# Window attention with a SoLU layer on one Trainium2 core: all turned rows in the weights' buffers, more load buffers, a new early list and new homes

## The chip, the cores and the metric

The kernel runs on one NeuronCore of a Trainium2 chip. The metric is the device time of one execution in microseconds; lower is better. Several runs are taken, and their median is quoted. Beside them stands one profiled execution, from which all rows below are read; its time is its own and need not be the median.

## What is computed

The reference is windowed causal attention (window 64, batch 8, 8 heads, sequence 576, head size 64), and its output, as 4608 tokens of 512 numbers, goes through a two-layer block with a softmax-weighted activation and a layer norm:

```python
scores = scale * np.matmul(q, k.transpose(0, 1, 3, 2))
mask = (rel >= 0) & (rel < window)
attn = softmax(np.where(mask, scores, -1e9))
x = np.matmul(attn, v)            # then rows of B*S tokens, 512 wide
h = x @ w_in                      # 512 -> 1024
sm = np.exp(h - h_max); sm = sm / (sm.sum(-1) + 1e-9)
solu = h * sm
ln = (solu - mu) / np.sqrt(var + 1e-6) * g_ln
out = ln @ w_out                  # 1024 -> 512
```

## The kernel before

The 4608 tokens are cut into 36 tiles of 128 rows. A tile t goes through these steps, named by letters in the list `START` and in `course`: S (scores, softmax over eight heads, and from tile 8 on the attention matrix turned by way of DRAM), T (for tiles below 8 the same turn on TensorE), X (attention times v), B (a power-of-two scale for the row block), h and H (the two halves of the product with w_in, then the statistics and the norm, then two 16-bit planes of the result that are stored to DRAM and come back turned by a transposing DMA), M (that turn on TensorE for the tiles that don't go by DMA), and O (the product with w_out and the store). I and G compute the weights' scales and split each 32-bit weight block into a high and a low 16-bit part.

Weights come as 64-bit numbers into the buffers "raw"; ACT and DVE rebuild 32-bit weights from them in eight blocks of tag "w" (`weight_block`): an ACT scaling, the low bits (on POOL or DVE), and two integer steps on DVE. Blocks 0 to 3 are w_in, 4 to 7 w_out. Tiles 0 to 2 multiply with the 32-bit w_in (L840), tile 0 also with the 32-bit w_out (L991). All later products use three 16-bit passes each (L852 for w_in, L1001 for w_out).

The order of instructions is made by a small planner (`Plan`) at build time. Each operation has an engine and an estimated cost; TensorE's operations follow the order of `START` and then of `course`, with those of tiles below `LOOSE` = 3 free to move. Buffers are rings (`RINGS`): an operation on a buffer waits until the earlier user of that slot is done. The planner runs the whole kernel forward by its estimates and writes one fixed order for each engine and for the DMA queue of SP. Ahead of the first output product it fills a share of the gaps that it foresees on TensorE with matmuls of no use (L1080, L1082).

`HOMES` says on which engine each movable operation of each tile runs, with the key (task, tile, part); from tile `LATER` = 14 on, even tiles use key 14 and odd ones key 15. Tasks: "low bits" and "high" for weights, "scale" (the softmax rows times the reciprocal sum; "ALL" is one DVE instruction for four heads), "soft" (the planes of the attention matrix), "join" (v rows of two tiles in one buffer; on SP it is a DMA from DRAM), "norm", "high planes" and "planes" (the two 16-bit planes of the normed rows), "tiny" (one-column arithmetic of the norm) and others. A key that is not listed takes a default, for example DVE for "planes" from tile 3 on and POOL below, ACT for "high planes" and POOL for "soft".

The turned rows of a tile live where `at_Y` says: tile 0 in its own buffer "yF", tiles below `FAR` in the ring "yT", the others in the ring "w" behind the eight weight blocks. `HALVES` names the tiles whose scores, transposes and values are cut into two pieces of four heads. The ring "pH" in PSUM has one buffer: a tile's product with w_in can't start until ACT's exponential and DVE's product (L876) of the tile before have read it. The largest |v| of a tile (L520 on DVE) needs the tile's v load.

Of the kernel before, what the change touches and what calls it, by code (L numbers as in the profile page):

```python
# [55 lines left out]
FAR = 8  # L56
# [16 lines left out]
    ("join", 8, 0): "POOL", ("join", 8, 1): "DVE", ("join", 9, 1): "DVE", ("join", 10, 0): "SP",
    ("join", 11, 0): "SP", ("join", 11, 1): "POOL", ("join", 12, 0): "SP", ("join", 12, 1): "DVE",
    ("join", 13, 1): "SP", ("join", 15, 0): "SP", ("low bits", 0, 0): "DVE", ("low bits", 2, 0): "DVE",
    ("low bits", 3, 0): "DVE", ("low bits", 6, 0): "DVE", ("norm", 0, 0): "DVE", ("norm", 0, 1): "DVE",
    ("norm", 1, 1): "DVE", ("norm", 2, 0): "DVE", ("norm", 3, 1): "DVE", ("norm", 5, 0): "DVE",
    ("norm", 6, 0): "DVE", ("norm", 9, 0): "DVE", ("norm", 10, 1): "DVE", ("norm", 11, 0): "DVE",
    ("norm", 11, 1): "DVE", ("norm", 13, 1): "DVE", ("norm", 14, 0): "DVE", ("norm", 14, 1): "DVE",
    ("norm", 15, 0): "DVE", ("norm", 15, 1): "DVE", ("planes", 1, 0): "DVE", ("planes", 2, 0): "DVE",  # L80
    ("planes", 2, 1): "DVE", ("planes", 3, 1): "POOL", ("planes", 4, 1): "POOL", ("planes", 5, 0): "POOL",
    ("planes", 5, 1): "POOL", ("planes", 6, 0): "POOL", ("planes", 7, 0): "POOL", ("planes", 7, 1): "POOL",
    ("planes", 8, 0): "POOL", ("planes", 8, 1): "POOL", ("planes", 9, 0): "POOL", ("planes", 10, 0): "POOL",
    ("planes", 10, 1): "POOL", ("planes", 11, 0): "POOL", ("planes", 12, 0): "POOL", ("planes", 13, 0): "POOL",
# [186 lines left out]
def tile_window_attention_solu_moe(  # L271
# [856 lines left out]
```

## Time and profile before

| | before |
|---|---|
| median of 3 runs | 500.72 us (500.54 to 501.61) |
| the profiled execution | 502.51 us |
| its span, from the first to the last instruction | 500.7 us |
| mean granted TensorE clock | 1.000 |
| TensorE busy | 490.8 us, 98% of the span |
| ACT, DVE, POOL busy | 375.5, 372.2, 174.5 us |
| DMA queue of SP: share of 16 engines | 82.0% |

The profile gives the busy time of each engine, which waits ended last before an instruction and by whom they were ended, and the chain of work that ended last. TensorE has a gap only where an input comes late; the filler matmuls count as busy.

### The profile page before, as it was taken

The numbers are of one execution on the slowest core, as the hardware profiler recorded it, in microseconds if no ns is written. First come the engines' busy times: TensorE is split into PE (matmuls) and PEld (weight loads), VectorE is DVE, ScalarE is ACT, GpSimd is POOL, SyncE is SP. The second block draws the span as 40 slices with busy tenths as digits, with TensorE's granted clock in tenths as the row PEclk, the third lists the DMA queues.
The fourth block names the chain that finished last, engine by engine and source line by source line (L and its number), as shares of the span: only waits on it lengthen the run. The fifth ranks groups of instructions, "written<-read, shape, count | busy, mean of one in ns | idle before, by whom it ended". The sixth has DMA issues, their size and how long they took to land.

```text
span 500.7 us, 12038 instructions
## 1 busy us (share of the span) xinstructions
PE 490.8 (98%) x4263; PEld 264.3 (53%) x4263; DVE 372.2 (74%) x1300; ACT 375.5 (75%) x1053; POOL 174.5 (35%) x302
## 2 busy tenths in 40 slices
PE   8999999989999999999999999999999999999997
PEld 7566654544555555545454545454545454444453
DVE  5998998888875869777778777788787887556440
ACT  4989999587977787988787878787878697543340
POOL 1255232534684342453333322232323242422100
PEclk9999999999999999999999999999999999999999
DMA  8982342769999999999999999999999999963311
GB/s 346 404 324 86 105 150 62 178 189 272 260 267 271 294 290 196 312 265 284 265 264 258 215 269 283 257 265 257 230 294 265 289 252 198 226 157 106 107 40 44
DMA packets 159292, 113.90 MB, mean 227 GB/s; under 512 B 130240, under 2 KB 130496, under 8 KB 158720
## 3 DMA queue, kind: packets, MB, share of 16 engines
q1 hardware_dynamic: 154912, 105.27, 82.0%
q10 hardware_dynamic: 4320, 7.87, 4.9%
q8 instruction: 33, 0.54, 0.5%
q14 instruction: 27, 0.22, 0.2%
HBM read 39.72 MB, written 41.42 MB: 162 GB/s over the span
## 4 chain that ended last, share of the span: by engine, by line
PE 80%; SPq 7%; DVE 5%; DMA 4%; issue 2%; ACT 1%; POOL 0%; POOLq 0%; ACTq 0%
PE pO L1001 28%; PE pH L852 27%; PE pS L671 5%; PE pX L808 5%; PE pH L840 4%; SPq L946 3%; SPq L754 3%; PE pX L1001 2%; DMA yd<-pl 2%; DMA yT<-yd 2%; PE pO_sums L448 2%; PE pO_x L808 2%; PE pO L991 1%; PE t L777 1%; PE t_s L671 1%
## 5 line engine op out<-in xcount | busy, mean ns | idle before, releaser
L852 PE MATMUL pH<-w_inH,xH 128*128 128x512 f16 x528 | 162.0, 379 | 0.4 <-DVE mst L888 0.4
L1001 PE MATMUL pO<-w_outH,w 128*128 128x512 f16 x416 | 128.1, 379 | 0.0
L852 PEld LDWEIGHTS <-xH 128*128 128x128 f16 x792 | 75.5, 98 | 90.4 <-issue 1.6
L692 ACT ACTIVATE sS<-sS,nmx 128x128 f32<-128x128 f32 x288 | 112.1, 398 | 7.3 <-DVE nmx L687 7.0
L1001 PEld LDWEIGHTS <-w 128*128 128x128 f16 x672 | 64.6, 98 | 77.5 <-issue 1.2
L852 PE MATMUL pH<-w_inL,xH 128*128 128x512 f16 x264 | 99.0, 379 | 0.0
L1001 PE MATMUL pO<-w_outL,w 128*128 128x512 f16 x208 | 78.8, 379 | 0.0
L873 ACT ACTIVATE e<-pH,mst,xscale 128x1024 f32<-128x1024 f32 x33 | 39.7, 1203 | 34.0 <-DVE mst L871 33.6
L867 DVE TENSOR_REDUCE mst<-pH 128x1 f32<-128x1024 f32 x36 | 44.0, 1222 | 24.7 <-PE pH L852 21.5
L692 ACT ACTIVATION_READ_ACCUMULATOR sS<-sS,nmx 128x1 f32 x288 | 56.7, 197 | 0.0
L876 DVE CUSTOM_DVE_ANT_0 e<-pH,e 128x1024 f32<-128x1024 f32 x36 | 44.0, 1222 | 10.4 <-ACT e L873 10.3
L937 POOL TENSOR_TENSOR pl<-e,pl 128x512 f16<-128x512 f32 x37 | 43.0, 1177 | 21.8 <-ACT pl L934 20.9
L880 ACT ACTIVATE unread<-e,mst 128x1024 bf16<-128x1024 f32 x36 | 41.2, 1144 | 11.3 <-DVE mst L879 10.7
L901 DVE TENSOR_SCALAR e<-e,mst 128x512 f32<-128x512 f32 x56 | 30.0, 573 | 20.4 <-POOL mst L896 18.7
L687 DVE CUSTOM_DVE_ANT_0 sS<-pS,maskNone 128x128 f32<-128x128 f32 x168 | 38.5, 286 | 7.4 <-PE pS L671 6.7
L895 POOL TENSOR_TENSOR mst<-mst,neghalf 128x1 f32<-128x1 f32 x36 | 20.1, 559 | 68.3 <-DVE mst L893 58.5
L1001 PE MATMUL pO<-w_outH,yT 128*128 128x512 f16 x112 | 34.5, 379 | 1.3 <-DMA yT<-yd 1.3
L823 ACT ACTIVATE xH<-pX,xscale 128x512 f16<-128x512 f32 x24 | 16.4, 685 | 25.5 <-PE pX L808 24.3
L743 POOL COPY raw<-sS 128x1024 uint16<-128x1024 uint16 x13 | 13.5, 1040 | 58.7 <-ACT sS L722 30.5
L722 ACT ACTIVATE sS<-sS,rec 128x128 f32<-128x128 f32 x96 | 31.5, 403 | 2.9 <-DVE mst L879 2.7
L671 PE MATMUL pS<-qk 64*64 64x128 f32 x864 | 30.8, 281 | 0.5 <-DVE nmx L687 0.5
L1012 ACT ACTIVATE ot<-pO,bound 128x512 f32<-128x512 f32 x33 | 22.5, 681 | 10.3 <-PE pO L1001 7.4
(142 smaller groups left out, 851.1 us busy)
## 6 DMA issues: line engine op xcount, KB each, us to landing
qk<-qk SPq DMA_DIRECT2D x36, 512.0 KB, 5.5
yd<-pl SPq DMA_DIRECT2D x33, 512.0 KB, 4.1
pd<-raw SPq DMA_DIRECT2D x28, 512.0 KB, 5.0
v<-vS SPq DMA_DIRECT2D x36, 256.0 KB, 4.0
y<-ot ACTq DMA_DIRECT2D x30, 256.0 KB, 4.5
raw<-w_in SPq DMA_DIRECT2D x4, 1024.0 KB, 9.5
raw<-w_out SPq DMA_DIRECT2D x4, 1024.0 KB, 8.2
vx<-vS SPq DMA_DIRECT2D x23, 128.0 KB, 3.7
```

Of the source, the lines that this page charges most:

```text
L671: nc.tensor.matmul(PS(t, r)[half * WIN:(half + 1) * WIN, p], q[rs, p, half * WIN:(half + 1) * WIN], keys, start=True, stop=True)
L687: plan.op("DVE", 213, lambda g=g: nc.vector.tensor_tensor_reduce(SS(t)[:, g], PS(t, g % 2)[:, g // 2], masks[first], scale=-SCALE, scalar=BIG,
L692: plan.op("ACT", 385, lambda g=g: nc.scalar.activation(SS(t)[:, g], SS(t)[:, g], AF.Exp, bias=cols("nmx", g), scale=-1.0, accum_out=cols(" ...
L722: plan.op(e, {"POOL": 355, "DVE": 200, "ACT": 300}[e], lambda g=g, e=e: nc.scalar.mul(SS(t)[:, g], SS(t)[:, g], rec()[:, g:g + 1]) if e == ...
L808: nc.tensor.matmul(PX(t)[r * D:(r + 1) * D, p, ks], (V if half else VX)(t)[:, h * D:(h + 1) * D], PT(t)[:, h, ks], start=True, stop=True)
L852: plan.op("PE", 216, lambda n=n, c=c, k=k, w=w: nc.tensor.matmul(PH(t)[:, hs], X(t, k)[:, c], w(c, h), start=(n == 0), stop=(n == len(pass ...
L867: plan.op("DVE", 1150, lambda: nc.vector.tensor_reduce(nmax(), PH(t), axis=AX.X, op=ALU.max, negate=True), [("pH", t)], [key(0)])
L873: plan.op("ACT", 1200, lambda: nc.scalar.activation(E(t), PH(t), AF.Exp, bias=nmax(), scale=XS(t, 2) if scaled else 1.0, accum_out=se()), ...
L876: plan.op("DVE", 1225, lambda: nc.vector.tensor_tensor_reduce(E(t), PH(t), E(t), scale=1.0, scalar=0.0, op0=ALU.mult, op1=ALU.add, accum_o ...
L880: plan.op("ACT", 1140, lambda: nc.scalar.activation(unread, E(t), AF.Square, bias=nmean(), scale=1.0, accum_out=ss()), H2 + [key(4)], [key ...
L937: plan.op(e, {"POOL": 1130, "DVE": 640}[e], lambda hs=hs, e=e: units[e].tensor_sub(PL(t)[:, 1, hs], E(t)[:, hs], PL(t)[:, 0, hs]), [("e", ...
L1001: plan.op("PE", 216, lambda f=f, i=i, x=x, k=k, y=y, w=w: nc.tensor.matmul(PO(), Y(t, y)[:, f], w(i, x), start=(f == k == 0), stop=(f == N ...
```

## The change

Four things are changed, all in the tables at the head of the kernel.

`FAR` goes from 8 to 1, so that the turned rows of all tiles but tile 0 lie in the "w" ring, and the ring "yT" is gone. The ring "qk" gets a fourth buffer, "v" a fifth and a sixth.

`HALVES` keeps tile 0 alone, and `START` is a new list of the first steps.

`HOMES` is made anew; about a hundred operations change their engine. By tile, the larger moves are: low bits of blocks 1, 4, 5, 7 from POOL to DVE, of block 6 from DVE to POOL; scale of tile 0's first four heads from ACT to one DVE instruction, of tile 3's second four from POOL to one DVE instruction; high of block 3's second half from ACT to DVE, of block 0's first half from ACT to POOL; planes of tile 1 (first half) and of tile 2 (both) from DVE to POOL; high planes of tile 2's first half from POOL to ACT. For the pairs of tiles from 14 on: join (14, 0) from ACT to SP; scale (14, 1) from DVE to ACT; soft (14, 0) from DVE to POOL and (14, 1) from ACT to DVE; high planes (15, 0) from POOL to DVE; norm (15, 0) from DVE to POOL; back and some tiny operations between DVE and POOL.

```diff
-HALVES = (0, 1, 2)
+HALVES = (0,)
 START = """
-S0 T0 X0 h0 H0 S1 I0 T1 X1 S2 S3 S4 B3 h1 H1 B4 T2 T3 B5 X2 h2 H2 X3 S5 T4 S6 G0 h3 S7 M0 X4 H3 T5 O0 h4 T6 O1
-H4 X5 S8 T7 B6 X6 h5 H5 O2 B7 X7 B8 S9 h6 B9 H6 S10 O3 S11 h7 X8 B10 S12 H7 O4 h8 H8 S13 B11 X9 O5 B12 h9 X10
-H9 O6 S14 h10 H10 S15 X11 O7 h11 X12 B13 H11 O8 S16 h12 H12 S17 X13 O9
+S0 S1 T0 X0 h0 H0 I0 S2 B3 T1 X1 S3 S4 h1 B4 T2 H1 X2 T3 h2 H2 B5 X3 S5 T4 G0 S6 h3 S7 M0 H3 X4 T5 O0 h4 T6 O1
+H4 X5 S8 T7 B6 X6 h5 H5 S9 O2 B7 B8 X7 h6 H6 S10 B9 O3 S11 X8 h7 H7 S12 B10 O4 h8 H8 X9 O5 S13 h9 B11 B12 X10
+H9 O6 h10 S14 H10 S15 X11 O7 h11 X12 H11 S16 O8 h12 B13 X13 H12 S17 O9
 """
...
-FAR = 8
+FAR = 1
...
 RINGS = {
-    "raw": 4, "w": 8, "qk": 3, "v": 4, "vx": 2, "sS": 3, "pd": 3, "PT": 2, "xH": 2,
-    "e": 3, "pl": 2, "yd": 4, "yF": 1, "yT": 3, "ot": 2, "nmx": 4, "sm": 4, "rec": 4, "mst": 6,
+    "raw": 4, "w": 8, "qk": 4, "v": 6, "vx": 2, "sS": 3, "pd": 3, "PT": 2, "xH": 2,
+    "e": 3, "pl": 2, "yd": 4, "yF": 1, "ot": 2, "nmx": 4, "sm": 4, "rec": 4, "mst": 6,
     "pS": 1, "pH": 1, "t": 2, "pX": 1, "pO": 1,
 }
```

## Rows read from the trace of the kernel before

**Rows 1.** Page, part 1: busy us, share of the span, instructions.
```profile
PE 490.8 (98%) x4263; PEld 264.3 (53%) x4263; DVE 372.2 (74%) x1300; ACT 375.5 (75%) x1053; POOL 174.5 (35%) x302
```

**Rows 2.** Busy time by stretch: PE, PEld, DVE, ACT, POOL, then clock, DMA, GB/s.
```profile
13.00:36.00 23.00, 22.32 (x254) 13.84 (x252) 20.87 (x77) 21.30 (x75) 9.13 (x19) 1.00 0.99 385
36.00:62.00 26.00, 25.86 (x225) 16.92 (x228) 22.94 (x67) 24.98 (x61) 10.60 (x16) 1.00 0.29 93
62.00:104.00 42.00, 39.32 (x342) 21.65 (x335) 37.51 (x123) 34.99 (x113) 15.30 (x30) 1.00 0.52 141
104.00:397.00 293.00, 293.00 (x2682) 153.23 (x2680) 227.20 (x847) 237.44 (x683) 114.10 (x188) 1.00 1.08 263
```

**Rows 3.** The same by stretch, of L1082 alone, then of L1080.
```profile
13.00:36.00 23.00, 2.21 (x16) 1.94 (x16) 1.00 0.99 385
36.00:62.00 26.00, 0.83 (x6) 0.75 (x6) 1.00 0.29 93
...
13.00:36.00 23.00, 1.41 (x16) 1.10 (x16) 1.00 0.99 385
36.00:62.00 26.00, 0.61 (x8) 0.53 (x8) 1.00 0.29 93
```

**Rows 4.** TensorE's waits: line, released by, us in total, times, longest.
```profile
PE pO L1001 <- DMA yT<-yd: 1.3, 1, 1.3
PE pO L991 <- DVE xscale L551: 1.1, 1, 1.1
...
PE pH L852 <- DVE mst L888: 0.4, 1, 0.4
```

**Rows 5.** DVE's waits, the one for v loads.
```profile
DVE vmost L520 <- DMA v<-vS: 8.4, 7, 3.8
```

**Rows 6.** Chain that ended last: start, us, what; up to 398 us.
```profile
393.27 3.00 DMA v<-vS
...
396.99 1.13 DVE e L876
```

**Rows 7.** Timeline of TensorE, tile 2's output product and the next scores.
```profile
103.00 0.39 PE L1001 MATMUL pO<-w_outH,yT 128*128 128x512 f16 x1 [1.27 <-DMA yT<-yd]
...
109.48 1.10 PE L671 MATMUL pS<-qk 64*64 64x128 f32 x32
```

**Rows 8.** Timeline of DVE: tile 2's planes.
```profile
87.21 1.63 DVE L937 TENSOR_TENSOR pl<-e,pl 128x512 f16<-128x512 f32 x2
```

**Rows 9.** Groups by line and form: busy us, mean ns of one, idle before.
```profile
L937 POOL TENSOR_TENSOR pl<-e,pl 128x512 f16<-128x512 f32 x37 | 43.0, 1177 | 21.8 <-ACT pl L934 20.9 <-DVE pl L934 0.4
L714 DVE TENSOR_TENSOR sS<-sS,rec 128x512 f32<-128x512 f32 x26 | 19.7, 757 | 0.7
L424 DVE TENSOR_SCALAR raw<-raw 128x1024 int32<-128x1024 int32 x4 | 2.9, 717 | 0.0
```

**Rows 10.** Timeline of SP's DMA queue: tile 2's transposing DMA.
```profile
95.04 5.90 SPq L946 DMA_TRANSPOSE yT<-yd  x1
```

**Rows 11.** Chain that ended last, ahead of tile 0's output product.
```profile
69.20 1.38 DVE pl L937
...
73.36 7.12 PE pO L991 x16
```

**Rows 12.** Timeline of DVE: the two longest gaps from 36 to 73 us, in brackets.
```profile
43.10 1.23 DVE L867 TENSOR_REDUCE mst<-pH 128x1 f32<-128x1024 f32 x1 [1.70 <-PE t_x L540]
55.99 1.23 DVE L867 TENSOR_REDUCE mst<-pH 128x1 f32<-128x1024 f32 x1 [0.92 <-PE pH L840]
```

**Rows 13.** Timeline of POOL: four scalings, twice.
```profile
23.47 3.43 POOL L723 TENSOR_SCALAR sS<-sS,rec 128x128 f32<-128x128 f32 x4 [3.30 <-DVE rec L706]
30.50 1.43 POOL L723 TENSOR_SCALAR sS<-sS,rec 128x128 f32<-128x128 f32 x4 [2.18 <-DVE rec L706]
```

**Rows 14.** One pair: DVE's timeline, then the chain on TensorE.
```profile
296.32 1.23 DVE L876 CUSTOM_DVE_ANT_0 e<-pH,e 128x1024 f32<-128x1024 f32 x1 [0.37 <-ACT e L873]
...
298.56 5.20 PE pH L852 x24
```

More of the change, by code (lines that the diff above doesn't have):

```diff
@@ new lines @@
+    ("PT", 1, 1): "DVE", ("PT", 4, 1): "ACT", ("PT", 5, 1): "ACT", ("PT", 6, 0): "DVE", ("PT", 7, 0): "DVE",
+    ("back", 1, 0): "DVE", ("back", 2, 0): "DVE", ("back", 6, 0): "DVE", ("back", 8, 0): "DVE",
+    ("back", 11, 0): "DVE", ("back", 14, 0): "DVE", ("high", 0, 0): "POOL", ("high", 3, 1): "DVE",
+    ("high", 5, 0): "POOL", ("high", 7, 0): "POOL", ("high planes", 1, 0): "POOL", ("high planes", 2, 1): "POOL",
+    ("high planes", 4, 0): "DVE", ("high planes", 6, 0): "POOL", ("high planes", 6, 1): "POOL",
@@ new lines @@
+    ("high planes", 7, 0): "POOL", ("high planes", 7, 1): "POOL", ("high planes", 9, 1): "POOL",
+    ("high planes", 10, 0): "POOL", ("high planes", 10, 1): "DVE", ("high planes", 11, 1): "DVE",
+    ("high planes", 13, 1): "POOL", ("high planes", 15, 0): "DVE", ("high planes", 15, 1): "POOL",
+    ("join", 0, 0): "ACT", ("join", 0, 1): "DVE", ("join", 1, 0): "ACT", ("join", 1, 1): "DVE",
+    ("join", 2, 0): "ACT", ("join", 2, 1): "ACT", ("join", 3, 1): "SP", ("join", 4, 0): "SP",
+    ("join", 4, 1): "SP", ("join", 5, 0): "SP", ("join", 5, 1): "ACT", ("join", 6, 0): "SP", ("join", 6, 1): "SP",
@@ new lines @@
+    ("join", 7, 0): "SP", ("join", 7, 1): "ACT", ("join", 8, 0): "SP", ("join", 8, 1): "DVE",
+    ("join", 9, 1): "DVE", ("join", 10, 0): "SP", ("join", 11, 1): "DVE", ("join", 12, 0): "SP",
+    ("join", 12, 1): "DVE", ("join", 13, 1): "SP", ("join", 14, 0): "SP", ("join", 15, 0): "SP",
+    ("low bits", 0, 0): "DVE", ("low bits", 1, 0): "DVE", ("low bits", 2, 0): "DVE", ("low bits", 3, 0): "DVE",
+    ("low bits", 4, 0): "DVE", ("low bits", 5, 0): "DVE", ("low bits", 7, 0): "DVE", ("norm", 0, 0): "DVE",
@@ new lines @@
+    ("norm", 0, 1): "DVE", ("norm", 1, 0): "DVE", ("norm", 2, 0): "DVE", ("norm", 3, 1): "DVE",
+    ("norm", 5, 0): "DVE", ("norm", 5, 1): "DVE", ("norm", 9, 0): "DVE", ("norm", 10, 0): "DVE",
+    ("norm", 10, 1): "DVE", ("norm", 11, 0): "DVE", ("norm", 11, 1): "DVE", ("norm", 12, 0): "DVE",
+    ("norm", 12, 1): "DVE", ("norm", 13, 0): "DVE", ("norm", 13, 1): "DVE", ("norm", 14, 0): "DVE",
+    ("norm", 14, 1): "DVE", ("norm", 15, 1): "DVE", ("planes", 3, 1): "POOL", ("planes", 4, 1): "POOL",
@@ new lines @@
+    ("planes", 5, 0): "POOL", ("planes", 6, 0): "POOL", ("planes", 7, 0): "POOL", ("planes", 9, 0): "POOL",
+    ("planes", 10, 0): "POOL", ("planes", 10, 1): "POOL", ("planes", 11, 0): "POOL", ("planes", 11, 1): "POOL",
+    ("planes", 12, 0): "POOL", ("planes", 12, 1): "POOL", ("planes", 13, 0): "POOL", ("planes", 14, 0): "POOL",
+    ("planes", 14, 1): "POOL", ("rec", 1, 0): "POOL", ("rec", 3, 0): "DVE", ("rec", 4, 0): "DVE",
+    ("rec", 6, 0): "DVE", ("rec", 9, 0): "DVE", ("rec", 10, 0): "DVE", ("rec", 13, 0): "DVE",
@@ new lines @@
+    ("rec", 14, 0): "DVE", ("rec", 15, 0): "DVE", ("rejoin", 0, 0): "POOL", ("rejoin", 2, 0): "ACT",
+    ("rejoin", 3, 0): "POOL", ("rejoin", 4, 0): "POOL", ("rejoin", 5, 0): "ACT", ("rejoin", 6, 0): "ACT",
+    ("rejoin", 7, 0): "ACT", ("rejoin", 8, 0): "ACT", ("rejoin", 9, 0): "POOL", ("rejoin", 11, 0): "ACT",
+    ("rejoin", 13, 0): "ACT", ("rejoin", 14, 0): "ACT", ("rejoin", 15, 0): "POOL", ("scale", 0, 0): "ALL",
+    ("scale", 0, 1): "ACT", ("scale", 1, 0): "POOL", ("scale", 1, 1): "POOL", ("scale", 2, 0): "ACT",
@@ new lines @@
+    ("scale", 15, 0): "ALL", ("scale", 15, 1): "ACT", ("soft", 4, 0): "DVE", ("soft", 4, 1): "DVE",
+    ("soft", 5, 1): "ACT", ("soft", 6, 1): "DVE", ("soft", 7, 0): "DVE", ("soft", 7, 1): "DVE",
+    ("soft", 8, 1): "DVE", ("soft", 9, 0): "ACT", ("soft", 9, 1): "ACT", ("soft", 10, 0): "ACT",
+    ("soft", 11, 1): "DVE", ("soft", 12, 0): "DVE", ("soft", 12, 1): "ACT", ("soft", 13, 0): "ACT",
+    ("soft", 13, 1): "DVE", ("soft", 14, 1): "DVE", ("soft", 15, 1): "ACT", ("store", 0, 0): "SP",
+    ("store", 2, 0): "SP", ("store", 3, 0): "SP", ("store", 4, 0): "SP", ("store", 8, 0): "SP",
@@ new lines @@
+    ("store", 10, 0): "SP", ("store", 13, 0): "SP", ("tiny", 0, 0): "POOL", ("tiny", 0, 2): "POOL",
+    ("tiny", 0, 3): "POOL", ("tiny", 1, 0): "POOL", ("tiny", 1, 2): "POOL", ("tiny", 1, 3): "POOL",
+    ("tiny", 3, 2): "POOL", ("tiny", 3, 3): "POOL", ("tiny", 4, 1): "POOL", ("tiny", 5, 0): "POOL",
+    ("tiny", 5, 2): "POOL", ("tiny", 5, 3): "POOL", ("tiny", 6, 2): "POOL", ("tiny", 7, 0): "POOL",
+    ("tiny", 7, 1): "POOL", ("tiny", 7, 3): "POOL", ("tiny", 8, 0): "POOL", ("tiny", 8, 2): "POOL",
```

61 lines of the change are left out of this document (9 added, 52 removed).

## The prediction

> **What bounds the kernel now.** I read the page's busy times first: TensorE is busy 490.8 of 500.7 us [rows 1]. A busy TensorE says little by itself, so the second view is its waits and the third is its busy time by stretch. From 104 to 397 us it has no gap at all, while DVE is busy 227.20 and ACT 237.44 of 293 us [rows 2]. That stretch cannot become shorter unless work leaves TensorE, and no matmul is added or removed by this change. What can move is the time before it, and any new gap in it.
>
> The fourth view shows that TensorE's early busy time is partly padding. The planner puts filler matmuls into the gaps that it foresees before the first output tile: 2.21 and 1.41 us of them between 13 and 36 us, 0.83 and 0.61 us between 36 and 62 [rows 3], 5.06 us together. Beside them stand true gaps: 62 to 104 us holds 42 less 39.32, so 2.68 us [rows 2], of which 1.3 is a wait for a turned tile, 1.1 a wait on DVE ahead of the first output product; and one wait of 0.4 us on DVE ahead of pH stands alone in the rest [rows 4]. So the removable part is at most about 5.1 + 2.7 + 0.4 = 8.2 us after 13 us, and what the kernel needs at that stage is DVE and ACT time: ACT is busy 24.98 and DVE 22.94 of the 26 us from 36 to 62, DVE 37.51 of 42 after that [rows 2].
>
> **The buffers.** FAR = 1 puts the turned rows of tiles 1 to 7 into the "w" ring. Tile 1 takes the slot of weight block 0, whose last readers (tile 2's first product and the split of the block) come before the turn of tile 1 on the same queues. Block 7's slot goes to tile 8, as before the change. The transposing DMA writes the same bytes into another place: I cost it at 0. Its bounds are 0 and, should a turn have to wait for a slot, the wait for a turned tile that the trace shows once, 1.3 us [rows 4].
>
> The memory freed buys one more "qk" and two more "v" buffers. DVE stood 8.4 us in seven waits for a v load at the head of its queue [rows 5]; most of it cost TensorE nothing, but the 0.4 us wait on pH [rows 4] is the end of such a chain: a v load under way from 393.27 for 3.00 us, then its maximum on DVE, and only then at 396.99 the product that frees pH [rows 6]. With two more tiles of v in flight I take this 0.4 as gone; bounds 0 to 0.4. qk loads were also held back for want of a slot, but no TensorE wait ends on a qk load, so the extra qk buffer is worth 0.
>
> **The order.** S9 now stands before O2. TensorE stood 1.27 us at 103.00 for tile 2's turned rows, and S9 (1.10 us, at 109.48 in the trace) ran after it [rows 7]. Done first, S9 covers about 1.03 us of that wait, by the time until the next piece starts. Against it: both plane subtractions of tile 2 go from DVE, where the pair took 1.63 us from 87.21 [rows 8], to POOL at 1.18 us each [rows 9]. POOL does them one after the other, 2.35 us instead of 1.63, 0.72 later if it begins at the same time; POOL also does only one cast instead of two (a cast goes to ACT), so it can begin earlier, and I take 0.35 later. The transpose went out only at 95.04, 5.90 us in its issue and behind loads on SP [rows 10], so a later store may also be hidden by that queue. Gain 1.03 - 0.35 = 0.68; ends 0 and 1.27. The other swaps in the list (B3 first, X4 after H3, S13 after O5) exchange pieces between places where TensorE had no gap: 0.
>
> S1 moves ahead of T0 and tiles 1 and 2 are no longer cut in halves. The early scores fill time in which filler stood, but tile 0's product waits for the weight blocks, which DVE makes. In 13 to 36 us DVE has 23 - 20.87 = 2.13 us idle [rows 2]. It gets block 1's low bits (0.72) and one scaling of four heads (0.76) [rows 9], 1.48 us; the small copies that come and go I let cancel. So the gap that the earlier S1 closes is filled again by what DVE takes on: 0, with ends of a gain of 3.6 us (all filler of that stretch [rows 3] given back) and a loss of 1.5.
>
> **The homes, from 36 to 73 us.** The wait of 1.1 us ahead of O0 [rows 4] ends a stretch in which DVE runs without a pause; in it stands a plane subtraction of tile 1, 1.38 us at 69.20, ahead of block 7's last step, and O0 begins at 73.36 [rows 11]. The change gives that subtraction to POOL. Taken alone this would let O0 begin 1.1 us earlier, and then it is TensorE's own work before it that is late: gain 1.07; ends 0 and 1.38.
>
> In the same stretch DVE takes on the low bits of blocks 4, 5 and 7 and loses block 6's: two more net, 2 x 0.72 = 1.43. It also takes a four-head scaling of tile 3 (0.76) and one high half of block 3 (no row on DVE; the nearest is 0.72) [rows 9]; together 2.9 us. DVE is idle 3.06 us from 36 to 62 [rows 2], and 1.70 and 0.92 of these are two single waits for TensorE at 43.10 and 55.99 [rows 12], 2.6 us, into which such work can go. So 2.9 - 2.6 = 0.3, and with some small operations that also come to DVE I take 0.5 us as exposed. Ends 0 and 2.9. ACT becomes lighter in exchange, but the waits above end on DVE, so I credit nothing.
>
> One rule of the Trainium skill speaks against handing plane subtractions to POOL. First the row: four scalings of POOL took 1.43 us at 30.50, and the same four took 3.43 us at 23.47, while DVE was at a weight block's integer steps [rows 13]. The Trainium skill, SBUF — State Buffer, section "Who interferes with whom", says that a DVE instruction with two SBUF inputs and a GpSimd instruction that reads SBUF exclude each other through the port that they share; the trace agrees. By the row's ratio the two subtractions would take 5.6 us instead of 2.35; that is a rival below.
>
> **The homes in the long stretch.** From tile 14 on each pair gives DVE less and POOL more work, and one half of the joined values of every even tile comes by a DMA instead of an ACT copy. The DMA engines show a share of 1.08 there and TensorE still never waits [rows 2], so I cost the DMA at 0. The tight place is pH: in the pair at 298 us DVE's product, which frees pH, starts at 296.32 and takes 1.23, and the next product into pH starts at 298.56 [rows 14], 1.0 us of margin. I cost the new homes there at 0; the ends are below (a rival). The end of the kernel, where TensorE runs without waits to the last product, stays.
>
> **The sum.** The profiled execution took 502.51 us, 500.7 of it span and 1.8 around; the median of the shown runs is 500.72, 1.8 less, and I apply the difference to it. -0.4 (v) - 0.68 (O2) - 1.07 (O0) + 0.5 (DVE) = -1.65: the profiled run would be 500.9 and the median 499.1 us.
>
> **The rivals.**
> First, the gains are given back: work that starts earlier at 73 us meets the same late turned tile at 103 us, since tile 2's planes hang on ACT and DVE and not on O0. Then O0's 1.07 reappears as wait ahead of O2, and only 0.4 or so is left: 500.3 us. For it speaks that both waits lie within 30 us with no filler between them; against it that ACT, which delays tile 2, loses work.
> Second, DVE becomes the bound of 36 to 73 us: if the 2.9 us come after 43 us, where DVE's remaining gap is 0.92 [rows 12], 2.0 us and more reach O0, whose gain is then gone too, and with the first 36 us also losing 1.0 the time is 500.72 + 2.0 + 1.0 - 1.1 (v and S9) = 502.6 us, slower. It decides from the point where the added DVE work exceeds the gaps it can reach.
> Third, POOL is held up by DVE: the two subtractions of tile 2 take 5.6 instead of 2.35 us, 3.3 more; O2 waits 1.27 - 1.03 + 0.35 + 3.3 = 3.9, 2.6 more than now, and with 1.5 gained elsewhere the time is 501.8 us. Against it: at that point (84 to 90 us) POOL has gaps and DVE's weight work is over.
> Fourth, the pH margin of 1.0 us breaks: one operation of 0.7 us more ahead of the product in every pair, with the small waits there, exceeds it by 0.3; nine pairs give 2.7 less the 1.65 gained: 501.8 us, up to 503.
> Fifth, the new list packs the early stretch better than I credit, and the filler of 13 to 36 us comes back: 499.1 - 2.6 = 496.5 us.
>
> **How the numbers follow.** A measurement of this kernel can tell about 0.2%, 1.0 us, from no change. Forecast 0.40 (own range 497.9 to 499.7), fifth rival 0.08, first 0.24, second 0.15, third 0.05, fourth 0.08. Faster: 0.40 + 0.08 = 0.48. Same: 0.24. Slower: 0.28. The range runs from 497.0, which leaves out most of the fifth, to 502.9, which leaves out the far ends of the second and fourth: 0.2 outside.
>
> **What would show it.** In the changed kernel's trace: TensorE's wait for a turned tile near 103 us below 0.7 us, S9 just ahead of it; no wait ahead of O0; no DVE wait for a v load; filler about as much as now; 104 to 397 us without gaps. If fillers fall by more than 2 us the fifth rival holds; if DVE from 36 to 73 has no gap and O0 starts after 73.4, the second; gaps repeating every 24.8 us would show the fourth. The prediction is wrong if the moved work leaves a stall in the long stretch, or if the planner's new order lengthens TensorE's path to O0.

## The result and the profile after

| | before | after |
|---|---|---|
| median, 20 runs of each beside one another | 500.99 us (499.24 to 507.94) | 505.24 us (504.43 to 507.43) |
| ratio to before, 95% interval | | 1.0094 [1.0081, 1.0107] |
| the profiled execution | 502.51 us | 506.04 us |
| its span | 500.7 us | 504.2 us |

The changed kernel is slower by 0.9%, where I forecast 0.3% faster. Each ratio here sets a kernel's executions beside those of the kernel before that were taken along with them, and leaves out those in a slower state that the chip shows now and then, so it need not be the ratio of two medians of this document. The changed kernel's lines are numbered one lower than before's from the tables on: L1000 is L1001 of before, L851 is L852, L519 is L520.

First the page's busy times, with the columns of [rows 1]:

```profile
PE 490.2 (97%) x4271; PEld 265.0 (53%) x4271; DVE 371.2 (74%) x1274; ACT 369.9 (73%) x1072; POOL 174.8 (35%) x284
```

And the busy times by stretch, with the columns of [rows 2]:

```profile
13.00:36.00 23.00, 22.40 (x264) 14.63 (x264) 22.13 (x78) 18.61 (x63) 6.22 (x18) 1.00 1.03 403
36.00:62.00 26.00, 26.00 (x222) 17.38 (x226) 23.65 (x68) 25.39 (x66) 9.01 (x13) 1.00 0.38 117
62.00:104.00 42.00, 39.49 (x367) 21.92 (x358) 38.52 (x125) 35.31 (x112) 19.69 (x30) 1.00 0.51 143
104.00:397.00 293.00, 288.86 (x2634) 150.92 (x2633) 223.86 (x818) 233.74 (x705) 112.69 (x174) 1.00 1.07 261
```

No engine became fuller: DVE and ACT lost a little of their time from 104 to 397 us, and the share of the DMA engines stood still at 1.07. Yet TensorE, which had no gap there [rows 2], now lacks 293 - 288.86 = 4.14 us. The waits say where: TensorE's, then those of DVE for v loads and of ACT for a transposing transfer (line, released by, us in total, times, longest):

```profile
PE pO L1000 <- DVE xH L823: 1.9, 1, 1.9
PE pH L851 <- DVE mst L887: 1.8, 1, 1.8
PE pO L990 <- DVE xscale L550: 1.7, 1, 1.7
...
PE pO L1000 <- DMA w<-yd: 0.4, 1, 0.4
PE pO L1000 <- issue: 0.4, 1, 0.4
...
DVE vmost L519 <- DMA v<-vS: 6.9, 4, 3.0
ACT sS L691 <- DMA raw<-pd: 3.1, 1, 3.1
```

The output products date the loss. Three starts of one (tile 10, tile 16, the last) from TensorE's timeline of before:

```profile
208.42 0.39 PE L1001 MATMUL pO<-w_outH,w 128*128 128x512 f16 x1
282.81 0.39 PE L1001 MATMUL pO<-w_outH,w 128*128 128x512 f16 x1
486.52 0.38 PE L1001 MATMUL pO<-w_outH,w 128*128 128x512 f16 x1
```

And the same three of after:

```profile
208.02 0.39 PE L1000 MATMUL pO<-w_outH,w 128*128 128x512 f16 x1
286.37 0.39 PE L1000 MATMUL pO<-w_outH,w 128*128 128x512 f16 x1
490.06 0.38 PE L1000 MATMUL pO<-w_outH,w 128*128 128x512 f16 x1
```

At 208 us the changed kernel is 0.40 us ahead; at tile 16 it is 3.56 behind, and at the end 3.54. The 0.40 comes from ahead of 15 us, where the first product with w_in began earlier. TensorE's timeline, before and after:

```profile
15.45 1.12 PE L840 MATMUL pH<-w,xH 128*128 128x512 f32 x2
15.01 1.13 PE L839 MATMUL pH<-w,xH 128*128 128x512 f32 x2
```

From there to the product at 208 us the two kernels take 192.97 and 193.01 us. (In the profiled executions of this document that first product starts from 15.19 to 15.50 us with the early order of before, and anywhere from 13.80 to 15.01 with that of the changed kernel; why it scatters there stays open.) So the early stretch, on which most of the forecast was spent, decides nothing, and two gaps of 1.94 and 1.79 us make 3.73 of the 3.96 us lost between tiles 10 and 16. The changed kernel's timeline (DVE and TensorE) at the first:

```profile
258.23 0.69 DVE L519 TENSOR_REDUCE vmost<-v 128x1 bf16<-128x512 f32 x1 [2.95 <-DMA v<-vS]
258.84 0.74 DVE L823 SCALAR_TENSOR_TENSOR xH<-pO_x,xscale,xH 128x512 f16<-128x512 f32 x1
259.63 0.38 PE L1000 MATMUL pO<-w_outH,w 128*128 128x512 f16 x1 [1.94 <-DVE xH L823]
```

The chain of waits ahead of the second, one piece of it:

```profile
264.55 5.21 DMA raw<-pd
```

And the timeline (ACT and TensorE) at the second:

```profile
269.84 0.34 ACTq L1017 DMA_DIRECT2D y<-ot  x1
270.23 0.40 ACT L691 ACTIVATE sS<-sS,nmx 128x128 f32<-128x128 f32 x1 [3.13 <-DMA raw<-pd]
277.16 0.39 PE L851 MATMUL pH<-w_inH,xH 128*128 128x512 f16 x1 [1.79 <-DVE mst L887]
```

In the first, DVE stands 2.95 us before the largest |v| of a tile that is needed much later, because the v load has not landed; behind it in DVE's fixed order waits the step that empties the PSUM bank pO, and O14 can't start. In the second, the output store of tile 14 on ACT's queue goes out only when a transposing transfer has landed at 264.55 + 5.21 = 269.76; ACT's softmax steps behind it start 3.13 us late, and the chain from there runs through DVE to the one buffer pH. Why should a store wait for a transposing transfer? A semaphore is the counter by which a transfer reports that it has landed. In the built program, and by the numbers that the instructions carry in the trace, the transfers of SP and ACT share eight of them in turn, and a transfer is held until its semaphore's last user has landed. For tile 14's store that user is now the transposing transfer at 264.55 us (the turn of tile 21's attention matrix), eight transfers earlier; in the kernel before it was a plain transfer issued 12 us ahead of the store.

What had changed for the transfers is in their table. From 208 to 382 us of before (operation, count, KB each, median us from issue to landing):

```profile
v<-vS SPq DMA_DIRECT2D x13, 256.0 KB, 4.2
vx<-vS SPq DMA_DIRECT2D x7, 128.0 KB, 4.4
w<-yd SPq DMA_TRANSPOSE x15, 6.6
```

And of after:

```profile
v<-vS SPq DMA_DIRECT2D x14, 256.0 KB, 6.8
vx<-vS SPq DMA_DIRECT2D x14, 128.0 KB, 3.2
w<-yd SPq DMA_TRANSPOSE x15, 8.3
```

The transfers of joined values, vx, doubled: that is the home join (14, 0), moved from ACT to SP. Loads of v land 2.6 us later and turned rows 1.7 us later.

### The profile page after: what moved, and what is told of

It is laid out like the page before. It is cut to its first block, busy times and chain, and to the rows that moved or that the text cites. A ratio compares the mean times of both kernels' runs of the same rounds, so it can differ in the third digit from the quotient of the medians.

```text
span 504.2 us, 12060 instructions
## 1 busy us (share of the span) xinstructions
PE 490.2 (97%) x4271; PEld 265.0 (53%) x4271; DVE 371.2 (74%) x1274; ACT 369.9 (73%) x1072; POOL 174.8 (35%) x284
## 4 chain that ended last, share of the span: by engine, by line
PE 86%; DVE 8%; DMA 3%; ACT 1%; issue 0%; SPq 0%; POOL 0%; ACTq 0%; POOLq 0%; DVEq 0%
PE pO L1000 32%; PE pH L851 30%; PE pS L670 5%; PE pX L807 4%; PE pH L839 4%; PE pX L1000 2%; PE pO_x L807 2%; DVE sS L686 2%; PE pO L990 1%; PE t_s L670 1%; PE pO_sums L447 1%; DMA v<-vS 1%; DVE e L875 1%; DMA w<-yd 1%; DMA raw<-pd 1%; ACT sS L691 1%
## 5 line engine op out<-in xcount | busy, mean ns | idle before, releaser
L1000 PE MATMUL pO<-w_outH,w 128*128 128x512 f16 x528 | 162.6, 379 | 2.8 <-DVE xH L823 1.9
L851 PE MATMUL pH<-w_inH,xH 128*128 128x512 f16 x528 | 162.1, 379 | 1.8 <-DVE mst L887 1.8
L1000 PEld LDWEIGHTS <-w 128*128 128x128 f16 x840 | 80.6, 98 | 99.2 <-issue 4.7
L851 PEld LDWEIGHTS <-xH 128*128 128x128 f16 x792 | 75.8, 98 | 91.6 <-DVE mst L875 1.9
L1000 PE MATMUL pO<-w_outL,w 128*128 128x512 f16 x264 | 100.0, 379 | 0.0
L851 PE MATMUL pH<-w_inL,xH 128*128 128x512 f16 x264 | 99.1, 379 | 0.0
L691 ACT ACTIVATION_READ_ACCUMULATOR sS<-sS,nmx 128x1 f32 x288 | 54.9, 191 | 0.0
L721 ACT ACTIVATE sS<-sS,rec 128x128 f32<-128x128 f32 x140 | 44.5, 390 | 3.8 <-DVE rec L705 2.3
L742 POOL COPY raw<-sS 128x1024 uint16<-128x1024 uint16 x25 | 26.0, 1039 | 58.7 <-ACT sS L721 29.6
L900 DVE TENSOR_SCALAR e<-e,mst 128x512 f32<-128x512 f32 x49 | 26.2, 561 | 15.5 <-POOL mst L895 14.2
L933 ACT CAST pl<-e 128x512 f16<-128x512 f32 x34 | 19.7, 614 | 22.0 <-DVE e L900 21.7
L890 POOL TENSOR_SCALAR mst<-mst,xscale 128x1 f32<-128x1 f32 x16 | 5.9, 366 | 72.9 <-ACT unread L879 44.9
```

The costliest lines, as they stand in the source:

```text
L691: plan.op("ACT", 385, lambda g=g: nc.scalar.activation(SS(t)[:, g], SS(t)[:, g], AF.Exp, bias=cols("nmx", g), scale=-1.0, accum_out=cols(" ...
L721: plan.op(e, {"POOL": 355, "DVE": 200, "ACT": 300}[e], lambda g=g, e=e: nc.scalar.mul(SS(t)[:, g], SS(t)[:, g], rec()[:, g:g + 1]) if e == ...
L851: plan.op("PE", 216, lambda n=n, c=c, k=k, w=w: nc.tensor.matmul(PH(t)[:, hs], X(t, k)[:, c], w(c, h), start=(n == 0), stop=(n == len(pass ...
L1000: plan.op("PE", 216, lambda f=f, i=i, x=x, k=k, y=y, w=w: nc.tensor.matmul(PO(), Y(t, y)[:, f], w(i, x), start=(f == k == 0), stop=(f == N ...
```

## The experiments

**Which part costs.** Five kernels take the change apart: all buffers alone, the list and the homes alone, and of the buffers each by itself.

```diff
 # buffers_alone: the kernel before with
-FAR = 8
+FAR = 1
-    ... "qk": 3, "v": 4, ... "yT": 3, ...
+    ... "qk": 4, "v": 6, ...
 # lists_alone: the changed kernel with FAR = 8, "qk": 3, "v": 4, "yT": 3
 # far_alone: the kernel before with FAR = 1 and no "yT"
 # v_buffers: far_alone with "v": 6;  qk_buffer: far_alone with "qk": 4
```

> The kernel before with FAR = 1 and the new rings (qk 4, v 6, no yT), but its own early list, halves and homes. Theory A (the loss is one DVE wait for a v load near 255 us, which stands there because the planner puts the maximum of |v| right behind a load that it believes to be landed, whatever the number of buffers): the planner's order changes with the rings, so a wait of DVE for v loads of some us stays, and the time is between 500 and 505 us depending on whether one of them meets a tight place. Theory B (the buffers bring their small gain and the new homes cost all of it): 500.3 to 500.9 us, no DVE wait for v loads.

> The changed kernel with the old rings (FAR = 8, qk 3, v 4, yT 3): new early list, halves and homes alone. Theory A: the wait at 255 us may vanish or move with the load order; the early stretch as in the changed kernel (tile 0's output product at 73.9, tile 2's at 103.7); 500 to 505 us. Theory B (the homes are what costs): 504 to 506 us, with gaps on TensorE of about 3.5 us in the long stretch.

> The kernel before with FAR = 1 and without the yT ring, nothing else: the turned rows of tiles 1 to 7 lie in the w ring, and every engine's and queue's order of instructions stays as it was. Prediction's step (costed at 0): 500.7 to 501.2, ratio 1.000. If a slot of the ring came free late: a longer wait of TensorE for a turned tile near 103 us, up to 502.

> The kernel before with FAR = 1 and six v buffers (qk stays at 3), old lists. Theory A (the planner puts the maximum of |v| right behind its load whatever the buffers, so more buffers only move the wait, and its order is upset): DVE waits for v loads stay above 8 us, and the time is 503 to 506. Theory B (more v buffers remove the waits; it is qk or the lists that cost): under 3 us of such waits, 500.3 to 500.9.

> The kernel before with FAR = 1 and the fourth qk buffer, v left at 4. My costing: an extra qk buffer is worth 0, 501 us. Theory of fitted orders: any ring that changes the order of SP's transfers costs, 502 to 505 us, with gaps of TensorE that end on DVE or ACT instructions standing behind transfers.

| kernel | median us (range) | ratio to before [95%] | DVE's waits for v loads |
|---|---|---|---|
| buffers_alone | 506.03 (503.69 to 509.39) | 1.0076 [1.0041, 1.0111] | 25.4 us, 12 times |
| lists_alone | 506.45 (503.36 to 508.79) | 1.0091 [1.0065, 1.0117] | 22.1 us, 13 times |
| far_alone | 501.40 (500.24 to 506.63) | 1.0025 [0.9988, 1.0063] | 1.3 us, 3 times |
| v_buffers | 504.60 (501.62 to 510.96) | 1.0074 [1.0042, 1.0107] | 16.9 us, 11 times |
| qk_buffer | 509.48 (503.13 to 511.57) | 1.0114 [1.0029, 1.0199] | 7.4 us, 6 times |

`FAR` alone costs nothing that can be told from no change, and its order on every queue is that of before. Each of the other parts alone costs about as much as the whole. They don't add up, so what costs is not a fixed price of each part. `buffers_alone`, `v_buffers` and `qk_buffer` lose without any of the new homes. The v buffers show best how. DVE's waits for v loads, where [rows 5] had 8.4 us, in `v_buffers`:

```profile
DVE vmost L520 <- DMA v<-vS: 16.9, 11, 4.3
```

and in `buffers_alone`:

```profile
DVE vmost L520 <- DMA v<-vS: 25.4, 12, 4.5
```

More buffers doubled and tripled the waits that they were to remove. One execution differs from another here as well: `far_alone` waited 1.3 us with the very order by which the kernel before waited 8.4, but 16.9 and 25.4 lie far beyond both. With a slot free, the planner asks for the load earlier and puts the maximum where it takes the load for landed, 1.63 us after its issue by its estimate; the rows above measured 4.2 to 6.8. Of `qk_buffer`, the profiled execution (503.13 us) had two gaps before pH, 2.5 us together; the three others took 509 to 512 us and have no trace, so their cause stays open; with four executions its interval reaches from 0.3 to 2.0%.

**The two gaps, one instruction at a time.** Four kernels move only single instructions of the changed kernel's finished order.

```diff
+LATE_MOST = {22: 19}     # one_max_later: the largest |v| of tile 22 behind tile 19's value planes
+LATE_MOST = {t: t - 1 - t % 2 for t in range(16, 32)}     # all_maxima_later
+LATE_STORE = {14: 18}    # store_later: tile 14's store behind tile 18's exponential
 # max_and_store_later: the first and the third
     order = plan.order()
+    for t, behind in LATE_STORE.items():
+        order.remove(stores[t])
+        order.insert(order.index(exps[behind]) + 1, stores[t])
```

> The changed kernel with one DVE instruction moved: the maximum of |v| of tile 22, on which DVE stood 2.95 us at 255, is issued behind the value planes of tile 19 instead of ahead of tile 18's. Nothing else differs on any engine or queue. Theory A: the wait of 1.9 us ahead of the output product at 259.6 is gone, and the wait of 1.8 us ahead of pH at 277 is gone too if it is its consequence: 501.5 to 502.0 us against 505.2. If only the first goes: 503.4. Theory C (the DMA queue is late as a whole and the next instruction waits as long): no change, 505.

> The changed kernel with the maxima of |v| of tiles 16 to 31 all issued behind the value planes of the pair before the one that needs them, where that is later than now; only DVE's order differs. Theory A: DVE's waits for v loads in the long stretch (3.0 and 4.0 us) go to 0, TensorE has no gap from 104 us on: 501.2 to 501.8 us. Theory C: as the changed kernel, 505.

> The changed kernel with two instructions moved: the maximum of |v| of tile 22 as before (one_max_later), and ACT's output store of tile 14 is issued behind the exponential of tile 18's product instead of 4.7 us earlier; on ACT it stood in that run until a transposing DMA had landed (5.6 us), and DVE and pH behind it. Theory D (two single instructions at the head of a queue, each waiting for a DMA): no gap of TensorE from 243 to 330 us, 501 to 502.5 us. Theory C (the DMA queues are late as a whole, and the next instruction in line waits as long): a gap of 2 to 4 us stays, 505 to 507.

> The changed kernel with one instruction moved, on ACT alone: the output store of tile 14 behind the exponential of tile 18 instead of in the middle of tile 22's softmax. Theory (the second stall comes from this store, whose semaphore was last used by the transposing transfer of tile 21's weights): ACT's 3.1 us wait and the 1.8 us gap of TensorE at 275 are gone, the 1.94 us gap ahead of O14 stays (it comes from a v load): 503.4 us. Rival (the landing of the transposing transfer itself holds the following tiles, whoever waits for it): the gap comes back within a few microseconds at a product that reads the turned weights, 505 us.

`one_max_later` took 507.39 us (505.77 to 509.72), ratio 1.0114 [1.0081, 1.0147]; `all_maxima_later` 509.34 (508.37 to 510.80, four executions), 1.0133 [1.0058, 1.0208]; `store_later` 505.62 (504.99 to 506.88, four executions), 1.0098 [1.0070, 1.0126]; `max_and_store_later` 502.80 (501.72 to 507.00), 1.0062 [1.0028, 1.0096]. The waits of `one_max_later`:

```profile
ACT sS L698 <- DMA raw<-pd: 5.6, 1, 5.6
PE pH L861 <- DVE mst L897: 4.2, 1, 4.2
```

and of `store_later`:

```profile
PE pO L1016 <- DMA v<-vS: 3.6, 1, 3.6
```

With the maximum out of the way the first gap is gone and the second has grown from 1.8 to 4.2 us, somewhat more than both together (3.73): the transposing transfer lands when it lands, and TensorE merely arrives at the stall earlier. That the median rose by 2.2 us goes with a lower clock of TensorE (last section). With the store out of the way the second is gone and the first is 3.6 instead of 1.9 us. The two lie in series, and mending one hands its gain to the other, so no single mend can show what either costs. With both out, neither gap is left, the median falls by 2.4 us and the ratio from 1.0094 to 1.0062. But the profiled execution of that kernel, its longest at 507.0 us, shows new gaps behind L833 (the step that is L823 above), 4.4 us together, with DVE waiting 13.1 us for v loads. `all_maxima_later` missed its forecast by more than 7 us: DVE still waited 5.4 us for v loads, where I expected 0, and a gap of 3.3 us stood at the second place. So single instructions are where late transfers are felt; why the transfers are late these runs don't show.

**The planner's estimate.** Here the planner is told that a v load of tile 14 and later lands 5.0 us after its issue.

```diff
+V_LANDS = 5000
-            plan.dma(P * P * 16, lambda: nc.sync.dma_start(V(t), ...), [], [("v", t)])
+            plan.dma(P * P * 16, lambda: nc.sync.dma_start(V(t), ...), [], [("v", t)], V_LANDS if t > 13 else 1630)
 # plan_v_late: in the changed kernel;  far_plan_v_late: in far_alone;  v_buffers_plan_v_late: in v_buffers
 # plan_v_late_store_later: with LATE_STORE as well
```

> The changed kernel; the planner is told that a v load of tile 14 and later lands 5.0 us after its issue instead of 1.63 (the traces show 3.0 to 6.75). TensorE's order is unchanged; some maxima on DVE and a few operations on ACT and SP move. Theory (queue heads that wait for transfers which the plan believes landed): DVE's waits for v loads fall from 6.9 us to below 4, the 1.94 us gap ahead of O14 goes; the second gap, which comes from a store on ACT behind a transposing transfer, can stay or move: 502 to 506 us. Rival (DVE and ACT are simply loaded too heavily there): both gaps stay in size, 505 us. Much below 503 would say that the v loads were the main cause.

> The kernel before with FAR = 1 and the same planned landing of 5.0 us for v loads from tile 14 on. The kernel with FAR = 1 alone has 1.3 us of DVE waits for v loads, and no TensorE gap in the long stretch. Theory: nothing to gain there, and 45 ACT operations and 93 DVE operations in new places can meet other transfers: 500.5 to 505 us, above 501.5 more likely than not, since every order that was not chosen on the chip has been slower so far. Rival (a better estimate of the landing gives a better order by itself): 499 to 501 us.

> The kernel with the six v buffers alone (504.6 us, 16.9 us of DVE waits for v loads), with the planned landing of 5.0 us. Theory (the ring's loss comes from maxima that stand behind loads which have not landed): DVE's waits for v loads fall below 8 us and at least 2 of the 3.5 us come back: 501 to 503 us. Rival (it comes from transfers on SP that now go out in another order, or from other queue heads): the waits fall, the time stays at 504 to 505 us.

> The changed kernel with v loads planned to land 5.0 us after their issue, and tile 14's store behind the exponential of tile 18 as well. With the planned landing alone DVE never waited for a v load, yet the time was 507.15 us: a gap of 4.6 us at 273 and a lower granted clock for 6 us after it (1.7 us). Theory: both stalls of the changed kernel are these two queue heads, so no gap is left from 104 us on, and 500.5 to 502.5 us remain. Rival (each order finds another stall, as the kernel with one maximum and the store moved did in its profiled execution): 503 us or more, with new gaps at other tiles.

`far_plan_v_late` took 501.30 us, 1.0007 [0.9970, 1.0045]: nothing to gain where TensorE never waited. (DVE's waits for v loads even rose there, from 1.3 to 5.3 us, and cost TensorE nothing.) `v_buffers_plan_v_late` took 503.20 (501.82 to 504.68), 1.0039 [1.0020, 1.0058]: no wait for a v load is left, TensorE has no gap from 104.7 us on, and what remains lies ahead of O0, which starts at 75.93 instead of 73.36 [rows 11]; part of that is a lower granted clock in this execution, 0.82 from 34 to 38 us and 0.75 from 38 to 42. So the late stalls of the v ring came from the maxima: without them the excess over the kernel before fell from 3.5 to 1.6 us. `plan_v_late` took 507.15 (four executions), 1.0107 [1.0070, 1.0144]. There too no wait for a v load is left, and the held store makes the only gap of the long stretch; two falls of the clock come on top (last section):

```profile
ACT sS L693 <- DMA raw<-pd: 6.0, 1, 6.0
PE pH L853 <- DVE mst L889: 4.6, 1, 4.6
```

`plan_v_late_store_later` took 502.90 (500.83 to 509.97), 1.0044 [1.0010, 1.0078]: four of ten executions at 500.83 to 501.78 us, as fast as before, the others 1 to 9 us longer than the kernel before. Removing both heads can be the whole cure, but not reliably; its longest execution, the profiled one, had gaps at other tiles (3.1 and 3.0 us).

**The doubled transfers.** The last three kernels put the one home back, add it alone to the kernel before, and put it back with the planned landing.

```diff
 # no_second_join_dma: the changed kernel with
-    ("join", 13, 1): "SP", ("join", 14, 0): "SP", ("join", 15, 0): "SP",
+    ("join", 13, 1): "SP", ("join", 15, 0): "SP",
 # far_second_join_dma: far_alone with ("join", 14, 0): "SP" added
 # no_second_join_plan_v_late: the first, with V_LANDS = 5000
```

> The changed kernel with one home put back: the second transferred half of the joined values of every even tile (from tile 14 on) is copied by ACT again, as in the kernel before. It takes 7 of 14 small vx transfers out of 208 to 382 us, where SP's queue is under way 168.2 of 174 us (156.8 in the kernel before) and a v load lands after 6.8 us in the median (4.2 before). Theory A (the added transfers fill SP's queue, everything behind them lands later): SP's time falls to 155 to 160 us, v loads land in 5 us or less, the stalls at 257 and 275 go, and no later one comes: 500 to 502.5 us. Theory B (the stalls are chance meetings of one order, whatever SP's load is): a new order with its own stalls, 503 to 506 us.

> The reverse: the kernel before with FAR = 1 (501.4 us, no gap from 104 us on, SP 149.5 of 174 us) and the one home of the changed kernel by which the second half of every even tile's joined values from tile 14 on comes by a transfer on SP instead of a copy on ACT. Theory A (SP's load): SP's time rises by 7 to 12 us in the same stretch, loads land later, and new gaps of TensorE appear: 503.5 to 506 us. Theory B: 501 to 502 us unless the new order happens on a stall.

> Both mends at once: the second join back on ACT, and the planned landing of v loads from tile 14 on at 5.0 us. Theory A: as without the planned landing, 500 to 502 us, with fewer waits of DVE for v loads; the best of the changed kernel's family, at best 0.5 us ahead of the kernel before, since up to 208 us the changed kernel is 0.4 us ahead of it. Theory B: 503 us or more.

The figures of SP's time in these expectations counted some instructions twice. Counted once, with each stretch of SP's timeline taken as one, SP's queue is under way 155 of the 174 us in the kernel before, 148 in `far_alone`, 160 to 162 in the changed kernel, 149 to 154 without the second join, 141 to 147 with the planned landing as well, and 162 in `far_second_join_dma`. (A range stands where neighbouring stretches can be joined or not.)

| kernel | median us (range) | ratio to before [95%] |
|---|---|---|
| no_second_join_dma | 502.01 (500.83 to 503.06) | 1.0004 [0.9970, 1.0037] |
| far_second_join_dma | 505.47 (500.42 to 509.44) | 1.0036 [0.9983, 1.0088] |
| no_second_join_plan_v_late | 501.01 (500.49 to 502.76) | 0.9975 [0.9931, 1.0018] |

Without the second join the loss is gone, with all the rest of the change in place. Busy time by stretch of `no_second_join_dma`:

```profile
104.00:397.00 293.00, 293.00 (x2656) 152.78 (x2655) 229.45 (x830) 241.93 (x722) 113.51 (x175) 1.00 1.05 264
```

Its longest wait of TensorE, and DVE's for v loads:

```profile
PE pO L990 <- DVE xscale L550: 1.7, 1, 1.7
DVE vmost L519 <- DMA v<-vS: 5.2, 5, 1.9
```

And its transfers from 208 to 382 us:

```profile
v<-vS SPq DMA_DIRECT2D x13, 256.0 KB, 6.0
vx<-vS SPq DMA_DIRECT2D x7, 128.0 KB, 3.6
w<-yd SPq DMA_TRANSPOSE x15, 7.6
```

TensorE is busy for all of 293 us again, and the longest wait for a v load is 1.9 us. ACT carries 8 us more than in the changed kernel (241.93 against 233.74) and nothing comes of it. A v load still takes 6.0 us, where I had expected 5 or less: transfers are early enough rather than quick. Three reservations stand. The planner makes a new order with each home, so this is not one instruction's doing alone. The reverse run points the same way, with nine of ten executions at 504 us and more, but its interval reaches below 1. And SP's time does not sort the kernels: it is 151 to 152 us in `buffers_alone`, `v_buffers` and `qk_buffer`, no more than before's, and they lose; it is 158 us in `far_plan_v_late`, and TensorE has no gap there from 104 to 397 us. With the second join the changed kernel loses under either planned landing (1.0094, 1.0107), and without it under neither (1.0004, 0.9975): so much is shown. Whether the transfers cost by filling SP's queue, or only through the orders that the planner makes with them, is not. The kernel with the home put back and the planned landing is the best of the family and can't be told from the kernel before, so even without the stalls no gain is shown.

**The wait ahead of O0.** One kernel tests whether the low bits that DVE took on set it.

```diff
 # low_bits_on_pool: the changed kernel, planned as it is, with the low bits of blocks 4, 5 and 7 issued on POOL
+        e = "POOL" if i in (4, 5, 7) else p
```

> The changed kernel with the low bits of weight blocks 4, 5 and 7 done by POOL at their place in the order, instead of by DVE (2.1 us less on DVE between 38 and 50 us); nothing else moves. If DVE's added work delays tile 0's output product (the prediction's second rival): the product starts 1 to 2 us earlier than 73.9, and the time is 1 to 2 us lower, 503.5 to 504.5. If the order of DVE's queue sets it (what stands ahead of the last weight step), the product starts within 0.4 us of 73.9, and the time stays at 505.

It took 508.21 us (four executions), 1.0149 [1.0110, 1.0188]; the wait ahead of O0 stayed at 1.73 us, and the two later gaps were 1.5 and 2.5 us. O0 started at 72.75, which by itself looks like the 1 us of my first branch, but this execution began earlier: from the first product with w_in to O0 it took 58.86 us, and the changed kernel 58.87. The low bits are not the cause. The rows of the next section show what stands there instead.

## Why the prediction was wrong, point by point

**The long stretch**, costed at 0, was the step that failed, and it cost 3.94 us in the profiled execution (from 0.40 ahead to 3.54 behind), which is 3.53 longer in all. I had the right object in hand (a transfer in place of ACT's copy) and priced it by the share of the DMA engines. That share was 1.08 before [rows 2] and 1.07 after; it doesn't tell how late a transfer lands. The table of transfers by landing time, and SP's timeline, did change, and I had not opened either for this stretch. "TensorE still never waits" described a stretch whose transfers just made it. The Trainium skill, Perfetto Trace Analysis, section "What 'DMA-bound' means", names the issuing engine's own track, solid with DMA instructions, as a bound of its own beside the DMA engines. SP's queue at 155 of 174 us before and 160 to 162 after comes near to that, and I had not weighed it; but 158 us without a gap in `far_plan_v_late` says that no such figure decides by itself.

**The v buffers**, -0.4, failed in their reason. I took a wait for a load to be a want of buffers. It was a want of distance between the load's issue and the instruction that reads it, and the planner uses a new buffer to move the load and its reader forward together. The 0.4 us wait at pH did go, and a wait of 0.4 us on issue at 387 us took its place. The qk buffer, costed at 0, is no better: alone it cost 1.1%, with the wide interval given above.

**O0**, -1.07, failed as well: the wait became 1.7 us, against 1.1 [rows 4]. The changed kernel's chain that ended last ahead of O0:

```profile
69.27 1.96 DVE w L428
71.23 1.14 DVE mst L866
...
72.43 1.13 DVE w L428
...
73.62 0.20 DVE bound L491
```

And its timeline of POOL beside it:

```profile
68.99 1.16 POOL L936 TENSOR_TENSOR pl<-e,pl 128x512 f16<-128x512 f32 x1
```

Tile 1's subtraction (1.38 us [rows 11]) left DVE as forecast. In its place came a second weight step, 1.13 us, and the first one took 1.96 instead of 1.13: 1.13 + 0.83 - 1.38 = 0.58 us later, against a start of O0 at 73.89 instead of 73.36, 0.53 later. Counted from the first product with w_in (15.01 and 15.45 us) O0 came 0.97 later, so some 0.44 us more was lost ahead of these rows; where, I have not found. The step that grew ran beside the very subtraction that had moved to POOL: they overlap from 69.27 to 70.15, 0.88 us, and it grew by 0.83. This fits the third rival's mechanism at another place; no run moved that subtraction alone. The rule that I cited for it (the Trainium skill, SBUF — State Buffer, section "Who interferes with whom": a DVE instruction with two SBUF inputs and a reading GpSimd instruction exclude each other) agrees with these rows. I had looked for it only at tile 2.

**Right:** `FAR` at 0, by a run of its own. The wait for turned rows ahead of O2 did fall, from 1.27 [rows 7] to 0.43 us, but that S9 did it is not shown: with the old list it was gone in `far_alone` and 0.43 us in `far_plan_v_late`. POOL's two subtractions of tile 2 took 2.72 us at 88.42, near the 2.35 that I took and far from the rival's 5.6. The first 36 us gave nothing: fillers from 13 to 62 us came to 7.0 us against 5.06 [rows 3], so the fifth rival falls (its 2.6 us is also less than the 3.6 us of filler in [rows 3], and the prediction doesn't say why). The second did not come from 36 to 62, where TensorE has no gap at all and DVE is idle for 2.35 us; the fourth came once, as a gap of 1.8 us before pH, not in every pair, and from a held store rather than from an added operation.

**Why the rivals did not save it.** All of them took the time of an engine as what decides. None asked which instruction at the head of a queue waits for a transfer, and what stands behind it, although [rows 5] and [rows 6] showed the pattern. The prediction named the outcome itself as what would make it wrong ("a stall in the long stretch"), but gave no price to it.

## What to carry to other kernels

Where the order of instructions is fixed at build time, judge an added transfer by when the transfers behind it land and by what stands behind each instruction that waits for them, not by the share of the DMA engines. Two stalls in series hide each other's price: remove both before you say what either costs. Another buffer helps a wait for a load only if the reader is also moved away from the load, so give the planner the landing time that the trace shows; here this removed the late stalls of the v ring, and alone it mended nothing in the changed kernel.

## What was not expected of the hardware

TensorE's clock fell after some of the long gaps, and not after others of the same length. Busy time by stretch in `plan_v_late`, around O0 (after a gap of 1.73 us) and after the gap of 4.6 us:

```profile
72.00:73.00 1.00, 0.18 (x1) 0.18 (x2) 1.00 (x6) 0.94 (x3) 0.90 (x2) 1.00 0.89 332
73.00:74.00 1.00, 1.00 (x2) 0.48 (x3) 1.00 (x10) 1.00 (x2) 0.18 (x1) 0.51 1.01 328
77.00:78.00 1.00, 1.00 (x3) 0.38 (x2) 1.00 (x2) 1.00 (x5) 0.00 (x0) 1.00 1.05 179
72.00:78.00 6.00, 5.18 (x8) 2.22 (x9) 6.00 (x25) 5.94 (x15) 2.26 (x4) 0.72 0.98 287
...
274.00:278.00 4.00, 0.00 (x0) 0.00 (x0) 3.75 (x6) 3.95 (x10) 2.08 (x2) 0.98 1.11 314
278.00:279.00 1.00, 0.81 (x2) 0.28 (x3) 0.93 (x8) 1.00 (x3) 0.00 (x0) 0.50 1.06 233
276.00:282.00 6.00, 3.81 (x11) 1.47 (x12) 4.13 (x14) 4.22 (x8) 2.19 (x4) 0.72 1.13 307
```

And in the changed kernel's profiled execution after its own 1.73 us gap ahead of O0:

```profile
72.00:78.00 6.00, 4.27 (x12) 1.97 (x11) 6.00 (x26) 5.92 (x13) 2.78 (x4) 1.00 0.94 262
```

After the engine has stood, the granted clock is 0.51 and 0.50 in the rows from 73 and from 278 us: half speed, 1.2 instead of 2.4 GHz. Over the 6 us from 72 and from 276 us its mean is 0.72, so each fall costs 0.28 x 6 = 1.7 us on top of the gap. In the profiled execution of the changed kernel the clock stayed at full speed, after gaps of 1.73, 1.94 and 1.79 us; why one gap of 1.73 us is followed by a fall and another isn't stays open.

This is part of why executions of one kernel lie apart. Of 25 executions of the kernel before that were taken beside `buffers_alone`, the five with a mean clock of 0.992 to 0.997 took 507.1 to 509.7 us, and the twenty with 0.998 to 1.000 took 499.9 to 503.6. It also fits that some kernels with one gap mended took longer than the changed kernel: all ten executions of `one_max_later` show 0.992 to 0.997, and fifteen of the changed kernel's twenty 0.999 or 1.000.
